# A fused attention and expert kernel: who stores the sums of w2, where 1e-6 is added, and which queue turns the last batch's x

## The chip, the cores and the metric

The kernel runs on one core of one Trainium2 chip. The metric is the device time of one execution in microseconds; the core has a matrix engine (TensorE, PE in the profile; its weight loads are listed apart as PEld), a vector engine (VectorE, DVE), an activation engine (ScalarE, ACT), a general engine (GpSimd, POOL) and a queue engine that only starts transfers (SyncE, SP). Everything is fp32, and the profile lists each fp32 matmul as two records.

## The reference

Two blocks follow each other. The first is an attention with polynomial features: `S1` and `S2` (8x32) project q and k, the outer product of the two 8-vectors gives 64 features, and no softmax is taken.

```python
def phi(x):
    a = np.einsum('rd,bhsd->bhsr', S1, x)
    b = np.einsum('rd,bhsd->bhsr', S2, x)
    return np.einsum('bhsi,bhsj->bhsij', a, b).reshape(*x.shape[:-1], r * r)
q_p, k_p = phi(q), phi(k)
kv = np.einsum('bhsf,bhsd->bhfd', k_p, v)
z = np.sum(k_p, axis=2)
num = np.einsum('bhsf,bhfd->bhsd', q_p, kv)
den = np.einsum('bhsf,bhf->bhs', q_p, z)[..., None] + 1e-06
x = (num / den)            # 4 batches, 4 heads, 1088 positions, 32 wide
```

The result, laid out as x with 4352 rows of 128, goes through a routed layer with 8 experts, in which every row meets every expert:

```python
logits = x @ w_gate; P = np.exp(logits - logits.max())
for _ in range(8):
    P /= P.sum(1, keepdims=True) + 1e-09
    P /= P.sum(0, keepdims=True) + 1e-09
    P *= N / E
for e in range(E):
    out += P[:, e:e + 1] * (np.maximum(x @ w1[e], 0.0) @ w2[e])
```

## The kernel before, in words

**Stages.** The attention of the four batches takes about the first 98 us, the routing (logits, then eight rounds of row and column sums on VectorE) some 106 to 175 us, and all the rest is expert work. Since the experts' products fill TensorE for most of the time, a generator `steps()` hands them out in small steps, and the attention and the routing call `fill(n)`, or yield `n`, at places where they would otherwise make TensorE wait: `n` is the amount of expert work put there, one unit being four matmul records of 480 columns. Up to the end of the routing, this work is on experts 0 and 1 without their routing weights, and the results stay in the tiles `kept`; they are multiplied by the weights later (`weigh_kept`). After the routing x is multiplied by an expert's weights before its first matmul (`prepare_x`, tile `xe`, on GpSimd).

**Expert work.** `items` lists pairs of a group of columns of x and an expert; an item is cut into `blocks`. In a block, `first` makes the hidden values (line 914, with the ReLU on ScalarE at 918), VectorE forms sums and differences of them (931 for groups of two tiles, 978 for groups of three), and `into` (1099) makes the second matmuls, eight steps later (`LAG`). Fast matrix multiplication saves matmuls: it needs sums of blocks of w2 as well, which GpSimd forms in `sums_of_two` (tile `ws`) and `sums_of_four` (tile `ws4`, line 242, ten instructions for 16 forms). An expert's `ws4` is formed once, stored in device memory (line 246, SyncE) and read back for later groups (line 230).

**Order.** On TensorE, VectorE, and for a part ScalarE, instructions run in the order in which the code states them. GpSimd and SyncE are ordered by the tile framework, except where `keep_in_program_order` holds an instruction in place. Each engine takes its queue in order, so a transfer on SyncE that waits for GpSimd holds up all SyncE's later transfers.

**Attention of batches 1 to 3.** `attention(b)` takes three chunks `c`. `times` multiplies the features of the queries (453), `tops(b, c)` makes numerators and denominators side by side in one PSUM tile `pn` (462), and `over(b, c)` takes the reciprocal of the denominators (475), multiplies (477) and transposes (481). In `tops`, two further matmuls (466) multiply 64 columns of ones with the tile `eps`, which holds 1e-6/128 everywhere, and so add 1e-6 to the 12 denominators of each row. `take_over` (486, 488) sends the quotient through device memory to turn it into `xT`, columns of x: one transfer out, four back. Batch 3 does this in two parts: positions 0 to 191 after `over(3, 1)` by GpSimd's queue, the rest after `over(3, 2)` by SyncE's. The logits (496) need all of `xT`.

Of the kernel before, what the change touches and what calls it, by code (L numbers as in the profile page):

```python
# [10 lines left out]
F32 = mybir.dt.float32  # L11
# [39 lines left out]
def kernel(  # L51
# [12 lines left out]
    nc = tc.nc  # L64
    P = nc.NUM_PARTITIONS
    B, H, S, D = q.shape
# [14 lines left out]
    consts = ctx.enter_context(tc.tile_pool(name="consts", bufs=1))  # L81
# [28 lines left out]
    ones = consts.tile([P, P], F32, name="ones")  # L110
# [34 lines left out]
        kvs.append(consts.tile([P, 2, 2, D + 1], F32, name=f"kvs{i}"))  # L145
        nc.gpsimd.memset(kvs[i], 0.0)

    eps = consts.tile([P, 3, H], F32, name="eps")
    nc.gpsimd.memset(eps, 1e-6 / P)

    v_slots = []
    for i in range(2):
        t = wk.tile([P, H + 1, NT + 1, D], F32, name=f"v{i}", bufs=1)
# [58 lines left out]
    stored, stored_four = {}, {}  # L212
# [13 lines left out]
    def sums_of_four(e, w2):  # L226

        ws = pools[0].tile([P, len(FORMS), FO // 4, H2], F32, tag="ws4", name="ws4")
        if e in stored_four:
            nc.sync.dma_start(out=ws, in_=stored_four[e])  # L230
            return ws

        def blocks(bs):
            b = w2[:, bs[0][1]::4, H2 * bs[0][0]:H2 * (bs[0][0] + 1)].unsqueeze(1)
            if len(bs) == 1:
                return b
            step = (bs[1][1] - bs[0][1]) * DM + (bs[1][0] - bs[0][0]) * H2
            return AP(tensor=b.tensor, offset=b.offset, ap=[b.ap[0], [step, 2], *b.ap[2:]])

        c = 0  # L240
        for ns, x, y, off in FOURS:
            tc.keep_in_program_order(nc.gpsimd.tensor_tensor(ws[:, c:c + len(ns)], blocks(x), blocks(y),  # L242
                                                             op=Alu.subtract if off else Alu.add))
            c += len(ns)
        stored_four[e] = dram.tile([P, len(FORMS), FO // 4, H2], F32, name=f"ws4{e}")
        nc.sync.dma_start(out=stored_four[e], in_=ws)
        return ws


# [205 lines left out]
    def tops(b, c):  # L455

        pn = bank()[:, 0:3 * H * (D + 1)].rearrange("p (t h d) -> p t h d", t=3, h=H)
        ph = third(phs[b % 2], c)
        for t in range(3):
            for i in range(2):  # L460
                for s in range(2):
                    nc.tensor.matmul(pn[64 * s:64 * (s + 1), t, 2 * i:2 * i + 2].rearrange("p h d -> p (h d)"),  # L462
                                     ph[:, i, s, 64 * t:64 * (t + 1)], kvs[b % 2][:, i].rearrange("p h d -> p (h d)"),
                                     start=(t == 0 and i == 0), stop=False, tile_position=(0, 64 * s))
        for s in range(2):
            nc.tensor.matmul(pn[64 * s:64 * (s + 1), :, :, D], ones[:, 0:64], eps, start=False, stop=True,
                             tile_position=(0, 64 * s))
        queries[b, c] = pn

    turned = {}  # L470
# [1 line left out]
    def over(b, c):  # L472
        pn = queries.pop((b, c))
        rc = wk.tile([P, 16], F32, tag="rc", name="rc")[:, 0:12].rearrange("p (t h) -> p t h", h=H)
        nc.vector.reciprocal(rc, pn[:, :, :, D])
        xs = wk.tile([P, 512], F32, tag="rd", name="rd")[:, 0:384].rearrange("p (h t d) -> p h t d", h=H, t=3)
        nc.vector.tensor_tensor(xs.rearrange("p h t d -> p t h d"), pn[:, :, :, 0:D],
                                rc.unsqueeze(3).to_broadcast([P, 3, H, D]), op=Alu.mult)
        if c == 0:
            turned[b] = wk.tile([P, H, W9], F32, tag="xt", name="xt", bufs=1)  # L480
        nc.vector.transpose(out=turned[b][:, :, 96 * c:96 * (c + 1)].rearrange("p h (t s) -> p h t s", t=3), in_=xs)
# [25 lines left out]
    def attention(b):  # L507


        follows = b + 1 < B  # L510
        keys_sums(b)
        times(b, 0)
        yield 2.2 if b == 1 else 2
        keys_kept(b)
        times(b, 1)
        tops(b, 0)
        if b == 1:
            transpose_q(2)
        yield 1.4
        times(b, 2)  # L520
        over(b, 0)
        tops(b, 1)
        if b == 1:
            queries_ab(2)
            repeat_a(2)
        if follows:
            repeat_b(b + 1)
        yield 1.4
        over(b, 1)
        if b + 1 == B:  # L530
            take_over(b, 0, 192, nc.gpsimd)
        yield 1.4
        tops(b, 2)
        if follows:
            transpose_k(b + 1)
        if b + 2 < B:
            load_k(b + 2)
            load_v(b + 2)
        yield 1.4
        over(b, 2)  # L540
        if b + 1 < B:
            take_over(b, 0, W9, nc.gpsimd)
        else:
            take_over(b, 192, W9, nc.sync)
        if follows:
            yield 0.7
            keys_ab(b + 1)
            yield 0.7
            if b == 1:
                transpose_q(3)  # L550
            keys_products(b + 1, 0)
            yield 1.4
            keys_products(b + 1, 1)
            if b == 1:
                queries_ab(3)
                repeat_a(3)
            yield 1.4
            keys_products(b + 1, 2)
            yield 1.4
# [10 lines left out]

    def routing():

        yield 5
        for c in range(len(chunks)):
            logits(c)
        yield 1
        for c in range(len(chunks)):
            logits_turned()
        lg = lgp[:, :, 0:E]
        mx = sk.tile([P, 1], F32, tag="mx", name="mx")  # L580
        nc.vector.tensor_reduce(out=mx, in_=lg, axis=AX.XY, op=Alu.max)
        yield 3
        pm = bank()[:, 0:P]
        for s in range(2):
            nc.tensor.matmul(pm[64 * s:64 * (s + 1)], mx.to_broadcast([P, 64]), ident, start=True, stop=True,
                             tile_position=(0, 64 * s))
        nc.vector.reduce_max(mx, pm, axis=AX.X)
        nc.vector.tensor_scalar(mx, mx, -1.0, 64 * math.log(2.0), op0=Alu.mult, op1=Alu.add)
        pw = p2s[0]
        nc.scalar.activation(out=pw[:, :, 0:E], in_=lg, func=Act.Exp, bias=mx[:, 0:1])  # L590

        step = 1.5 * 2.0 ** (23 - 149 + 64)
        nc.vector.tensor_scalar(pw[:, :, 0:E], pw[:, :, 0:E], step, step, op0=Alu.add, op1=Alu.subtract)
        for it in range(ITERS):
            rs = sk.tile([P, SA], F32, tag="rs", name="rs")
            nc.vector.reduce_sum(rs, pw, axis=AX.X)  # L596
            nc.vector.reciprocal(rs, rs)
            p1 = p1s[it % 2]
            nc.vector.scalar_tensor_tensor(p1[:, 0:SA], rs.unsqueeze(2).to_broadcast([P, SA, E]), UP,
                                           pw[:, :, 0:E], op0=Alu.mult, op1=Alu.mult)  # L600
            cs = sk.tile([P, E], F32, tag="cs", name="cs")
            nc.vector.reduce_sum(cs, p1.rearrange("p g e -> p e g"), axis=AX.X)  # L602
            yield 4.25
            pc = bank()[:, 0:E]
            for s in range(2):
                nc.tensor.matmul(pc[64 * s:64 * (s + 1)], ones[:, 0:64], cs, start=True, stop=True,
                                 tile_position=(0, 64 * s))
            cr = sk.tile([P, E], F32, tag="cr", name="cr")
            nc.vector.reciprocal(cr, pc)
            last = it == ITERS - 1  # L610
            pw = lgp if last else p2s[(it + 1) % 2]
            nc.vector.scalar_tensor_tensor(pw[:, :, 0:E], cr.unsqueeze(1).to_broadcast([P, SA, E]),
                                           float(N) / E * (1.0 if last else UP), p1[:, 0:SA],
                                           op0=Alu.mult, op1=Alu.mult)

        nc.vector.transpose(out=lgT.rearrange("p a s -> p (a s)"), in_=lgp.rearrange("p a e -> p (a e)"))
        for b in (1, 0, 2, 3):
            nc.sync.dma_start(out=pT[:, b * S:(b + 1) * S],
                                                  in_=lgT[32 * b:32 * b + E].rearrange("p a s -> p (a s)"))
# [489 lines left out]
    def steps():  # L1109

        todo, sums_at, t = {}, {}, 0
        for k in range(len(blocks) + 5):
# [5 lines left out]
            if k < len(blocks):  # L1118
# [11 lines left out]
                if q == 1 and j + 1 < first_weighted and not direct_of(j + 1) and loaded_w[j + 1][2] is None:  # L1130
                    w1, w2, _ = loaded_w[j + 1]
                    w = w1, w2, sums_of_two(items[j + 1][1], w2)
                    loaded_w.update({i: w for i in loaded_w if items[i][1] == items[j + 1][1]})
                if q == 0:
                    if weighted and 1 <= es.index(e) <= es[0] + 1:
                        weigh_kept(g, es.index(e) - 1)
                if k == len(blocks) - HELD:
                    kept_to_sums(g)
                m, step, sums_ = (four if tiles == 3 else two)(k)
# [131 lines left out]
```

## Time and profile before

| what | value |
|---|---|
| time, median of 3 (lowest to highest) | 920.12 us (920.08 to 920.75) |
| span of the profiled execution | 918.0 us |
| busy: PE, PEld | 911.2 us, 637.4 us |
| busy: DVE, ACT, POOL | 678.9 us, 421.6 us, 204.0 us |
| mean traffic of the transfers | 140 GB/s |
| granted TensorE clock | full in nearly all slices |

A busy share says how long an engine had at least one instruction in it. Matmuls overlap in the engine, so the distance from one start to the next says more on TensorE than the duration of one. The chain of waits follows the work that ended last back to its start; the waits list for each engine what ended its idle time.

### The profile page before, as it was taken

The page shows a single profiled execution, that of the slowest core. Times are in us where ns is not written, and L with a number is a line of the kernel's source. Part 1 is how long each engine was busy: PE and PEld are TensorE (multiplying, and loading weights), DVE is VectorE, ACT ScalarE, POOL GpSimd, SP SyncE. Part 2 cuts the span into 40 slices and gives each one's busy share as a digit, 9 for nine tenths or more (in the row PEclk, how much of TensorE's full clock was granted, in tenths as well). Part 3 has the DMA queues.
Part 4 walks back from the last instruction along what each step waited for, and adds up shares of the span by engine and source line. Part 5 has one row for each costly group of instructions (what it writes and reads, how often), then busy time and mean ns, then how long its engine had stood idle before and what let it go on. Part 6 is the DMA issues. An engine that isn't in the chain of part 4 may idle for free.

```text
span 918.0 us, 18893 instructions
## 1 busy us (share of the span) xinstructions
PE 911.2 (99%) x7442; PEld 637.4 (69%) x7442; DVE 678.9 (74%) x1173; ACT 421.6 (46%) x915; POOL 204.0 (22%) x212
## 2 busy tenths in 40 slices
PE   9999999999999999999999999999999999999997
PEld 6777544466666677777777777777777655556886
DVE  7678699888776798666975656956567976758665
ACT  3455555554444454444544444544445444445443
POOL 3121100175545421201210010110100243210220
PEclk9999999999999999999999999999999999999999
DMA  9994100213454535534364343454445456453640
GB/s 254 308 273 163 54 1 1 70 64 127 148 150 139 186 119 174 165 110 150 114 185 134 117 143 112 132 187 127 133 122 165 130 170 195 162 166 92 177 153 13
DMA packets 91305, 128.15 MB, mean 140 GB/s; under 512 B 25392, under 2 KB 69504, under 8 KB 86480
## 3 DMA queue, kind: packets, MB, share of 16 engines
q1 hardware_dynamic: 88384, 121.42, 42.7%
q0 software_dynamic: 1600, 5.36, 2.1%
q8 instruction: 58, 0.95, 0.4%
q10 hardware_dynamic: 1232, 0.16, 0.1%
q14 instruction: 31, 0.25, 0.1%
HBM read 107.88 MB, written 19.05 MB: 138 GB/s over the span
## 4 chain that ended last, share of the span: by engine, by line
PE 97%; DVE 2%; ACT 1%; issue 0%; POOL 0%; DVEq 0%; POOLq 0%
PE a L914 51%; PE s L1099 41%; PE a L347 1%; PE a L462 1%; PE a L114 1%; DVE hb L931 1%; PE a L314 0%; PE s L376 0%; PE a L426 0%; PE s L392 0%; DVE cs L602 0%; PE a L496 0%; PE a L392 0%; ACT hb L918 0%; DVE rs L596 0%
## 5 line engine op out<-in xcount | busy, mean ns | idle before, releaser
L914 PE MATMUL a<-xe,w 128*64 128x256 f32 (+1 forms) x2560 | 569.8, 470 | 0.0
L918 ACT ACTIVATE hb<-a 128x256 f32<-128x256 f32 (+4 forms) x408 | 195.0, 480 | 241.5 <-PE a L914 209.3
L914 PEld LDWEIGHTS a<-xe,w 128*64 128x64 f32 x2560 | 263.0, 137 | 50.8 <-issue 1.8
L918 ACT ACTIVATE hx<-a 128x256 f32<-128x256 f32 (+1 forms) x360 | 167.3, 465 | 213.5 <-PE a L914 191.6
L1099 PE MATMUL s<-hb,ws 128*64 128x256 f32 (+3 forms) x1312 | 256.1, 395 | 0.2 <-DVE hb L931 0.2
L1099 PE MATMUL s<-hx,ws 128*64 128x256 f32 x1280 | 233.9, 379 | 0.0
L978 DVE TENSOR_TENSOR hb<-hb 128x512 f32<-128x512 f32 (+1 forms) x204 | 133.5, 664 | 102.8 <-ACT hb L918 98.8
L978 DVE TENSOR_TENSOR hx<-hx 128x512 f32<-128x512 f32 (+1 forms) x204 | 149.8, 744 | 65.0 <-ACT hx L918 60.2
L1099 PEld LDWEIGHTS s<-hb,ws 128*64 128x64 f32 x1312 | 134.9, 137 | 87.8 <-issue 64.5
L678 POOL TENSOR_TENSOR xe<-xT,xe 128x768 f32<-128x768 f32 (+2 forms) x41 | 80.3, 1958 | 481.2 <-DMA xe<-pT 377.0
L1099 PEld LDWEIGHTS s<-hx,ws 128*64 128x64 f32 x1280 | 132.7, 137 | 71.6 <-issue 50.3
L914 PE MATMUL a<-xT,w 128*64 128x416 f32 (+3 forms) x512 | 119.7, 462 | 0.0
L1099 PE MATMUL s<-hb,w 128*64 128x256 f32 (+3 forms) x536 | 114.2, 408 | 0.0
L1099 PE MATMUL s<-hx,w 128*64 128x256 f32 x384 | 76.0, 379 | 0.0
L931 DVE TENSOR_TENSOR hb<-hb 128x416 f32<-128x416 f32 (+7 forms) x84 | 60.7, 723 | 18.0 <-ACT hb L918 14.0
L1099 PEld LDWEIGHTS s<-hb,w 128*64 128x64 f32 x536 | 54.1, 137 | 19.0 <-issue 6.5
L914 PEld LDWEIGHTS a<-xT,w 128*64 128x64 f32 x512 | 48.9, 137 | 25.5 <-issue 15.7
L242 POOL TENSOR_TENSOR ws<-w 128x256 f32<-128x256 f32 (+1 forms) x70 | 60.5, 899 | 8.1 <-DMA w<-in_moe_w_dram 5.2
L931 DVE TENSOR_TENSOR hx<-hx 128x256 f32<-128x256 f32 (+1 forms) x65 | 39.5, 612 | 24.0 <-ACT hx L918 22.8
L1099 PEld LDWEIGHTS s<-hx,w 128*64 128x64 f32 x384 | 40.8, 137 | 6.6
L978 DVE TENSOR_TENSOR pqg<-hb 128x512 f32<-128x512 f32 x68 | 40.5, 637 | 0.0
L978 DVE TENSOR_TENSOR pqg<-hx 128x512 f32<-128x512 f32 x68 | 35.0, 554 | 0.0
(181 smaller groups left out, 485.0 us busy)
## 6 DMA issues: line engine op xcount, KB each, us to landing
w<-in_moe_w_dram SPq DMA_DIRECT2D x82, 512.0 KB, 5.5
ws<-ws SPq DMA_DIRECT2D x34, 1024.0 KB, 5.0
xe<-pT SPq DMA_DIRECT2D x34, 384.0 KB, 4.1
ws<-ws SPq DMA_DIRECT2D x12, 512.0 KB, 3.6
ph<-qa SPq DMA_DIRECT2D x12, 288.0 KB, 4.7
rb<-qb SPq DMA_DIRECT2D x3, 1152.0 KB, 7.2
pb<-pT SPq DMA_DIRECT2D x6, 384.0 KB, 8.3
kx<-in_k_dram SPq DMA_DIRECT2D x4, 544.0 KB, 4.0
```

The costliest lines, as they stand in the source:

```text
L114: nc.tensor.matmul(warm[:, 0:P], ones, ones, start=True, stop=True)
L242: tc.keep_in_program_order(nc.gpsimd.tensor_tensor(ws[:, c:c + len(ns)], blocks(x), blocks(y), op=Alu.subtract if off else Alu.add))
L347: nc.tensor.matmul(pv[64 * s:64 * (s + 1), i], kp[0:n, H * t + h].rearrange("p i j -> p (i j)"), vx[0:n, slots[h], t, :], start=(t == 0 an ...
L462: nc.tensor.matmul(pn[64 * s:64 * (s + 1), t, 2 * i:2 * i + 2].rearrange("p h d -> p (h d)"), ph[:, i, s, 64 * t:64 * (t + 1)], kvs[b % 2] ...
L678: tc.keep_in_program_order(nc.gpsimd.tensor_tensor(out, x, pb, op=Alu.mult))
L914: nc.tensor.matmul(ph[sl], loaded_w[j][0][:, P * f + H2 * s:P * f + H2 * (s + 1)], sources[j][:, lo:hi], start=True, stop=True, tile_posit ...
L918: nc.scalar.activation(out=out, in_=ph, func=Act.Relu)
L931: nc.vector.tensor_tensor(out, a, b, op=Alu.subtract)
L978: nc.vector.tensor_tensor(out if not isinstance(out, tuple) else places(*out), places(*a), places(*b) if isinstance(b, tuple) else b, op=A ...
L1099: nc.tensor.matmul(sums[g][i][H2 * s:H2 * (s + 1), n * place:n * (place + 1)], w, x, start=c == 1, stop=c == per, tile_position=(0, H2 * s))
```

## The change

Four things change. The tile `eps` and the matmuls with it go, and `over` adds 1e-6 with a VectorE instruction before the reciprocal. The store of `ws4` moves from SyncE's queue to GpSimd's, held in program order, so that SyncE doesn't wait for GpSimd's sums. `weigh_kept` is asked for one block later in an item (at `q == 1` instead of `q == 0`), so that its transfer and its product come behind the preparation of the next item. The first part of batch 3's x goes by SyncE's queue; the expert work between `tops(3, 2)` and `over(3, 2)` shrinks from 1.4 to 0.6 units, and that ahead of the logits grows from 5 to 6.

```diff
-    eps = consts.tile([P, 3, H], F32, name="eps")
-    nc.gpsimd.memset(eps, 1e-6 / P)
...
-        nc.sync.dma_start(out=stored_four[e], in_=ws)
+        tc.keep_in_program_order(nc.gpsimd.dma_start(out=stored_four[e], in_=ws))
...
-                                     start=(t == 0 and i == 0), stop=False, tile_position=(0, 64 * s))
-        for s in range(2):
-            nc.tensor.matmul(pn[64 * s:64 * (s + 1), :, :, D], ones[:, 0:64], eps, start=False, stop=True,
-                             tile_position=(0, 64 * s))
+                                     start=(t == 0 and i == 0), stop=(t == 2 and i == 1), tile_position=(0, 64 * s))
...
-        nc.vector.reciprocal(rc, pn[:, :, :, D])
+        nc.vector.tensor_scalar_add(rc, pn[:, :, :, D], 1e-6)
+        nc.vector.reciprocal(rc, rc)
...
         if b + 1 == B:
-            take_over(b, 0, 192, nc.gpsimd)
+            take_over(b, 0, 192, nc.sync)
...
-        yield 1.4
+        yield 1.4 if follows else 0.6
         over(b, 2)
...
-        yield 5
+        yield 6
         for c in range(len(chunks)):
             logits(c)
...
-                if q == 0:
-                    if weighted and 1 <= es.index(e) <= es[0] + 1:
-                        weigh_kept(g, es.index(e) - 1)
+                if q == 1 and weighted and 1 <= es.index(e) <= es[0] + 1:
+                    weigh_kept(g, es.index(e) - 1)
```

## The prediction

> **What bounds the kernel now.** I read the page first, then the chain of waits in order of time, then the waits of TensorE alone. The page's first part and its chain name one engine:
>
> ```profile
> PE 911.2 (99%) x7442; PEld 637.4 (69%) x7442; DVE 678.9 (74%) x1173; ACT 421.6 (46%) x915; POOL 204.0 (22%) x212
> ...
> PE 97%; DVE 2%; ACT 1%; issue 0%; POOL 0%; DVEq 0%; POOLq 0%
> ```
>
> A busy share of 99% alone isn't proof, since overlapping matmuls can hide slow starts. So I look at start distances in the chain:
>
> ```profile
> 317.88 0.86 PE a L914 x4
> 319.17 0.86 PE a L914 x4
> 320.89 0.86 PE s L1099 x8
> 322.62 0.86 PE a L914 x4
> ```
>
> From 317.88 to 319.17 lie 12 records of 256 columns: 1.29 us, 107.5 ns each. From 317.88 to 322.62, the pattern's period, are 44 such records, 4.74 us, 107.7 ns each. The distance stays the same for 500 us, whatever the other engines do. So TensorE starts the next matmul when its array takes one, and only fewer or shorter matmuls shorten this stretch. The waits of TensorE over the whole run say where it does stand still:
>
> ```profile
> PE a L114 <- POOL own L116: 1.0, 1, 1.0
> PE a L392 <- ACT kvz L362: 0.6, 1, 0.6
> PE s L1099 <- DVE hb L931: 0.2, 1, 0.2
> ```
>
> The first two come in the first 15 us, which the change doesn't touch; the third, at 166 us, is all the visible idle time that an earlier partner could give back. Busy time by stage agrees (the columns are the stretch, its length and the busy time of each engine with its instructions, PE first):
>
> ```profile
> 25.00:110.00 85.00, 85.00 (x1070) 61.92 (x1066) 64.04 (x111) 39.83 (x101) 14.55 (x25) 1.00 0.69 209
> 110.00:184.00 74.00, 73.78 (x468) 33.52 (x466) 65.34 (x118) 43.95 (x91) 4.02 (x4) 1.00 0.09 23
> 184.00:317.00 133.00, 133.00 (x999) 86.97 (x996) 101.87 (x144) 58.94 (x121) 74.65 (x78) 1.00 0.41 130
> 317.00:836.00 519.00, 519.00 (x3955) 374.90 (x3952) 374.83 (x657) 230.43 (x478) 91.34 (x58) 1.00 0.47 146
> ```
>
> TensorE lacks 0.22 us between 25 and 836 us. Stalls below what this view shows are found from start distances: about 0.15 us ahead of the logits at 106.1, 0.11 behind them, 0.05 at 139.6. I put everything recoverable after 25 us at 0.3 to 0.9 us.
>
> **What the Trainium skill says.** "Perfetto Trace Analysis", section Identifying the Most-Contended Engine, warns that matmul busy time is no measure of how near an engine is to its peak; hence the step by start distances above. "VectorE: DVE Perf Modes", section The TRN2 errata, prices a matmul at max(60, 6+FD) cycles of 2.4 GHz: 109 ns for 256 columns, which the measured 107.5 ns fits, and 25 ns for the 12 columns of the `eps` product. Its VectorE row has 120 fixed cycles of 0.96 GHz for a PSUM source and 58 for an SBUF source. "DMA: Bandwidth & Descriptors", section Anatomy of one DMA, gives about 2.0 us plus bytes over 436 GB/s for a transfer issued by GpSimd: for the 1 MiB of `ws4` an estimate of 4.4 us; the trace has 4.7 to 5.1 us for the store by SyncE.
>
> **Part 1, the eps matmuls.** Nine calls of `tops` (three batches by three chunks), two matmuls each, two records per matmul: 36 records leave TensorE. Their busy time in the timeline contains latency that overlaps the next matmul, so I take start distances again:
>
> ```profile
> 34.74 0.24 PE L466 MATMUL a<-eps,ones 128*64 128x12 f32 x4
> 34.83 0.63 PE L914 MATMUL a<-xT,w 128*64 128x256 f32 x4
> ```
>
> Four records occupy 0.09 us here, and 0.09 us again at 37.34 to 37.43; the median distance behind such a record is 28 ns, or 0.11 us for four. Nine times 0.09 to 0.11 is 0.8 to 1.0 us; the sum of all distances behind the 36 records is 1.03 us. TensorE has no idle time around them to absorb the gain, so it goes to the end: minus 1.0 us. The memset of `eps` (0.12 us on GpSimd at 2.5 us) hides beside the warm-up matmuls.
>
> **Part 2, VectorE's addition.** The trace has the same pair of instructions in batch 0, and the present reciprocal from PSUM:
>
> ```profile
> 26.72 0.17 DVE L405 TENSOR_SCALAR rc<-rd 128x9 f32<-128x9 f32 x1
> 26.93 0.22 DVE L406 RECIPROCAL rc<-rc 128x9 f32<-128x9 f32 x1
> 97.11 0.23 DVE L475 RECIPROCAL rc<-a 128x12 f32<-128x12 f32 x1
> ```
>
> There the addition takes a distance of 0.21 us, from SBUF; from PSUM a little more, at most the 0.25 us of the old reciprocal to its successor. The reciprocal now reads SBUF, slightly cheaper. I take 0.23 us more per `over`, 2.1 us on VectorE for nine, three of them (0.7 us) in each batch. Queued behind the longer `over` are sums for expert blocks (931), transposes and products of the next keys (302, 331). VectorE is full in 65 to 80 us (4.8 of each 5 us), so there the 0.7 us stays until the gap of 2.73 us at 84 to 86.7, where it ends. Who waits meanwhile: the key matmuls (314) start at 75.1, some 1.7 us after their transposes end at 73.4; the key sums (347) at 82.8, 1.6 us after the product ends at 81.2. TensorE itself comes about 0.6 us earlier, so the slack falls to 0.3 us or so, and stays positive. Cost: zero; bounds 0 and 2.1 us, if every addition reached TensorE.
>
> **Part 3, batch 3's x.** Now the second part's outward transfer starts on SyncE at 98.58, its returns at 101.19 to 102.94, and TensorE's queue passes its waits for them by 104.3; the logits start at 106.11. So there is 1.8 us of slack. Afterwards the first part's quotient is ready near 94.3 (94.46 now; TensorE gains 0.7 us by then and VectorE loses 0.5). One outward transfer of 2.6 to 3 us and four returns of 0.44 us of SyncE's time put it at 99. `over(3, 2)` moves ahead by up to 0.8 units of 0.8 us, 0.64 us; its quotient comes near 98 and waits for SyncE until 99. The same steps as before, 2.6, 1.75 and 2.1 us, end near 105.1. The logits are due at 106.11 less 1.0 plus 0.2 units (0.16 us): 105.25. It just fits. Cost 0; bounds 0 and 1 us. The order of the work changes, not its amount: the units that are shifted are expert work that has to be done anyway.
>
> **Part 4, the stores.** SyncE's waits name what is relieved:
>
> ```profile
> SPq L246 <- POOL ws L242: 111.4, 7, 17.0
> ```
>
> Seven stores, 111 us of SyncE standing behind GpSimd's sums, between 175 and 308 us, in front of loads of `xe` and weights. Yet TensorE loses nothing to it in this stretch (133.00 of 133.00 us). The gain is slack alone: zero. GpSimd gets about 0.5 to 1 us more for each store (its queue's transfers at line 486 take 0.59 to 0.73 us). Behind each stands the next weighing of `xe`, which waits 6 to 8.5 us for its transfer now, and then the next sums. The tightest place is 240 us: `xe` is ready at 240.2, its item begins about 241, for 236.27 to 238.2 went to the kept product. Since `weigh_kept` moves behind and the load is no longer held up, this widens. In the last group, the kept products move by one block (4.7 us) and still end well ahead of their use. Zero.
>
> **Sum.** 920.12 - 1.0 = 919.1 us.
>
> **The rivals.** (a) The small stalls go as well: up to 0.9 us more, 918.2 to 918.6. For it: 0.2 us at 166 us hangs on the place of routing work between sums, which the shift by 0.2 units changes. Against it: the same shift can make such stalls. (b) A wait takes the removed matmuls' place: x arrives late at the logits (up to 1 us), or the additions reach TensorE (up to 2.1 us): 919.7 to 921.5, say 920.5. For it: slack of only 0.1 to 0.3 us in both reckonings. Against it: 1.8 us of slack before, and the greater lead of `over(3, 2)`. (c) GpSimd becomes the bound from 184 to 317 us: with its slack below 1 us at the tightest item, a store that took 1.5 us and stalled 0.6 us in each of seven items gives plus 4.2, 923.3 us, slower than before. Against it: GpSimd is busy 74.65 of 133 us there, and it waits for transfers between its pieces.
>
> **How the numbers follow.** The forecast, 918.6 to 919.7, has 0.62; (a) 0.12, (b) 0.18, (c) 0.08. The range takes (a) nearly whole and (b) to near its middle: 918.2 to 920.9. Faster by over 0.2% means under 918.28 us: half of (a), 0.07. Slower means over 921.96: (c) and the end of (b), 0.09. Within 0.2%: 0.84.
>
> **What would show it.** No line with `eps`; the records of PE down by 36; PE still without idle time from 25 to 836 us; the start of the logits near 105.3 us; nine additions on DVE; SyncE's wait for `ws` gone and its loads earlier. Wrong would be: a gap in front of the logits, matmuls at 75 or 83 us waiting for DVE, a wait of TensorE for GpSimd after 184 us, or a steady distance other than 107.7 ns.

## The result, and the profile after

The kernel after takes 926.00 us (median of 6 runs, 924.15 to 926.72), beside it the kernel before 920.13 us (919.50 to 920.75): 1.006 times as long, 95% interval 1.0047 to 1.0073. The forecast was 919.1 us with a range of 918.2 to 920.9, so the 5.9 us have to be explained. The profiled executions span 924.2 and 918.0 us, both at full clock.

The first and fourth parts of the page of the kernel after (busy time, and the chain that ended last by engine):

```profile
PE 913.0 (99%) x7406; PEld 534.1 (58%) x7406; DVE 688.9 (75%) x1182; ACT 421.4 (46%) x915; POOL 202.6 (22%) x213
...
PE 90%; DVE 5%; DMA 3%; issue 1%; SPq 0%; ACT 0%; ACTq 0%; DVEq 0%
```

TensorE has 36 records less, as foreseen, and its share is still 99%. But the chain now leaves it: 97% PE before, 90% now. The chain runs over VectorE and transfers for 8% of the span, so these end waits of TensorE; the 8% is the way back along the chain, not lost time. The waits of TensorE say which (engine, line, what it waited for: total, times, longest):

```profile
PE s L1094 <- DVE hx L973: 2.5, 2, 2.2
PE a L114 <- POOL own L116: 1.0, 1, 1.0
PE a L389 <- ACT kvz L359: 0.6, 1, 0.6
PE a L491 <- issue: 0.5, 1, 0.5
PE a L909 <- DVE rd L472: 0.4, 1, 0.4
PE a L311 <- DVE kT L301: 0.3, 1, 0.3
PE a L459 <- ACT hb L913: 0.3, 1, 0.3
```

The second and third are the start's, known from before. That of line 311 lies at 20.4 us, ahead of the first changed instruction of the attention, and that of line 459 at 34.6 us stands in kernels without the eps edit too (0.5 us in e2 below). The others come with the change. (Lines of the kernel after stand 3 to 5 lower than before: 1094 was 1099, the second matmuls; 973 was 978, VectorE's sums; 491 was 496, the logits; 459 was 462, `tops`; 472 was 477, the multiplication in `over`; 243 was 246, the store.) The same by stage, columns as in the prediction:

```profile
25.00:110.00 85.00, 83.61 (x1018) 61.59 (x1015) 63.77 (x116) 39.03 (x99) 11.61 (x20) 1.00 0.70 208
110.00:184.00 74.00, 73.79 (x467) 33.27 (x461) 63.83 (x119) 43.57 (x90) 0.14 (x1) 1.00 0.11 28
184.00:317.00 133.00, 130.53 (x968) 70.89 (x964) 108.55 (x142) 57.38 (x119) 77.08 (x87) 1.00 0.36 127
317.00:836.00 519.00, 519.00 (x3950) 283.59 (x3948) 376.26 (x652) 229.81 (x475) 93.39 (x57) 1.00 0.46 145
```

Nothing is lost after 317 us: TensorE is busy for all 519 us and its steady distance is unchanged (107.8 ns for 256 columns before, 107.7 after, over the whole stretch). It stands still for 2.5 us between 184 and 317 us, where it lost nothing before, and for 1.4 us before 110 us. Milestones place the loss in the same way. The logits start at 107.65 us (106.11 before), the matmul of the first sum over columns at 125.05 (121.61), the first matmul on weighted x at 187.41 (184.21), the last matmul at 918.69 (912.65). So 1.5 us are lost up to the logits, 1.7 to 1.9 at them and just behind, and nearly 3 after the routing. How many of the first 1.5 us belong to the change can't be told from this: the same attention starts the logits at 106.11 to 107.44 us in the kernel before, e2, e5, e6 and e9 below, and that of the kernel after at 105.90 in e4.

**The largest wait.** The timeline of the kernel after around its only 2.2 us wait (start, duration, engine, line, operation; in brackets the idle time before and its releaser):

```profile
195.33 0.60 POOL L243 DMA_DIRECT2D ws<-ws  x1 [0.30 <-POOL ws L239]
195.82 7.71 DVE L736 TENSOR_TENSOR z<-x,z 128x384 f32<-128x384 f32 x1 [1.93 <-ACT x L745]
195.95 1.82 POOL L673 TENSOR_TENSOR xe<-xT,xe 128x768 f32<-128x768 f32 x1
197.73 6.10 POOL L239 TENSOR_TENSOR ws<-w 128x256 f32<-128x256 f32 x10
204.44 0.65 PE L1094 MATMUL s<-hx,ws 128*64 128x256 f32 x4 [2.25 <-DVE hx L973]
```

One VectorE instruction takes 7.71 us. In the kernel before the same instruction took 0.56 us (at 192.62). It reads two SBUF operands and begins while GpSimd issues the store that the change gave it. GpSimd then works through a weighing and ten sums without slowing down (1.82 and 6.10 us), and VectorE's instruction ends only during the last of these. VectorE's next sums are what line 1094 waits for. So it isn't GpSimd that TensorE waits for here, but VectorE, which stands behind GpSimd.

### The profile page after: what moved, and what is told of

The parts are those of the page before. It is cut to its first block, busy times and chain, and to the rows that moved or that the text cites. A ratio compares the mean times of both kernels' runs of the same rounds, so it can differ in the third digit from the quotient of the medians.

```text
span 924.2 us, 18839 instructions
## 1 busy us (share of the span) xinstructions
PE 913.0 (99%) x7406; PEld 534.1 (58%) x7406; DVE 688.9 (75%) x1182; ACT 421.4 (46%) x915; POOL 202.6 (22%) x213
## 4 chain that ended last, share of the span: by engine, by line
PE 90%; DVE 5%; DMA 3%; issue 1%; SPq 0%; ACT 0%; ACTq 0%; DVEq 0%
PE a L909 48%; PE s L1094 41%; DVE hb L926 1%; DMA rb<-qb 1%; DMA kx<-in_k_dram 1%; DVE z L736 1%; DMA v<-in_v_dram 1%; PE a L344 0%; PE a L459 0%; DVE kT L299 0%; PE a L491 0%; DVE hx L973 0%; DVE rd L472 0%; DVE ph L450 0%; DVE w L736 0%
## 5 line engine op out<-in xcount | busy, mean ns | idle before, releaser
L909 PE MATMUL a<-xe,w 128*64 128x256 f32 (+1 forms) x2560 | 516.3, 470 | 0.0
L909 PEld LDWEIGHTS a<-xe,w 128*64 128x64 f32 x2560 | 200.1, 137 | 86.6 <-issue 1.6
L1094 PE MATMUL s<-hb,ws 128*64 128x256 f32 (+3 forms) x1312 | 228.6, 395 | 0.2 <-DVE hb L926 0.2
L1094 PE MATMUL s<-hx,ws 128*64 128x256 f32 x1280 | 205.4, 379 | 2.5 <-DVE hx L973 2.5
L973 DVE TENSOR_TENSOR hx<-hx 128x512 f32<-128x512 f32 (+1 forms) x204 | 160.2, 795 | 58.2 <-ACT hx L913 53.1
L1094 PEld LDWEIGHTS s<-hb,ws 128*64 128x64 f32 x1312 | 104.7, 137 | 116.3 <-issue 86.6
L1094 PEld LDWEIGHTS s<-hx,ws 128*64 128x64 f32 x1280 | 102.4, 137 | 103.4 <-issue 74.5
L1094 PE MATMUL s<-hb,w 128*64 128x256 f32 (+3 forms) x536 | 107.1, 408 | 0.0
L1094 PE MATMUL s<-hx,w 128*64 128x256 f32 x384 | 67.9, 379 | 0.0
L1094 PEld LDWEIGHTS s<-hx,w 128*64 128x64 f32 x384 | 33.2, 137 | 11.5
```

The costliest lines, as they stand in the source:

```text
L909: nc.tensor.matmul(ph[sl], loaded_w[j][0][:, P * f + H2 * s:P * f + H2 * (s + 1)], sources[j][:, lo:hi], start=True, stop=True, tile_posit ...
L973: nc.vector.tensor_tensor(out if not isinstance(out, tuple) else places(*out), places(*a), places(*b) if isinstance(b, tuple) else b, op=A ...
L1094: nc.tensor.matmul(sums[g][i][H2 * s:H2 * (s + 1), n * place:n * (place + 1)], w, x, start=c == 1, stop=c == per, tile_position=(0, H2 * s))
```

## The experiments

Each was measured beside the kernel before, whose median was 920.04, 920.27 and 920.07 us in the three sets (36 to 49 runs). They fall into four groups.

**One part at a time.** The kernel before with one part of the change:

```diff
e1_eps_alone
-    eps = consts.tile([P, 3, H], F32, name="eps")
...
-            nc.tensor.matmul(pn[64 * s:64 * (s + 1), :, :, D], ones[:, 0:64], eps, start=False, stop=True,
...
+        nc.vector.tensor_scalar_add(rc, pn[:, :, :, D], 1e-6)
+        nc.vector.reciprocal(rc, rc)
e2_store_alone
+        tc.keep_in_program_order(nc.gpsimd.dma_start(out=stored_four[e], in_=ws))
e3_x_alone
+            take_over(b, 0, 192, nc.sync)
...
+        yield 1.4 if follows else 0.6
...
+        yield 6
```

> The kernel before with the eps matmuls replaced by VectorE's addition, nothing else. Theory A (the attention stage is paced by its transfers, rb above all, and by VectorE, so that the 1.0 us that TensorE saves turns into waits there): 920.0 to 921.7 us, with new gaps of TensorE at the products with the features (34, 64 and 67 us) and behind the key matmuls (78 us). Rival B (TensorE sets the pace here, the late rb of the changed kernel's profile was an accident of the transfers): 919.1 us, no such gaps.

> The kernel before with the store of ws4 on GpSimd's queue, nothing else. Theory A (a store in GpSimd's queue ahead of a weighing and ten sums lets GpSimd keep SBUF to itself, and a VectorE sum stands until the last of them is done): one VectorE instruction of over 3 us between 184 and 320 us, TensorE waiting 2 to 3 us for it, 922.5 to 923.5 us. Rival B (that stall came from where the earlier delay of 3 us had put VectorE against GpSimd, the store has no part in it): 920.1 us, within 0.3.

> The kernel before with batch 3's first part on SyncE's queue and the shifted units, nothing else. Theory A (the second part's transfer waits in SyncE's queue for the returns of the first and then lands after the logits are due): 921 to 922 us, TensorE standing 0.7 to 1.8 us inside the logits. Rival B (the logits stall in the changed kernel only since the attention stage was late there): 919.8 to 920.4 us, no gap at the logits.

And the kernel after with its store back on SyncE:

```diff
e4_after_store_back
-        tc.keep_in_program_order(nc.gpsimd.dma_start(out=stored_four[e], in_=ws))
+        nc.sync.dma_start(out=stored_four[e], in_=ws)
```

> The changed kernel with the store of ws4 back on SyncE's queue. Theory A: the 2.9 us at 204 to 208 us go, no VectorE instruction over 3 us after 184 us: 922.8 to 923.4 us. Rival B (the collision comes from the phase): a stall of the same kind stays, 925.5 to 926.5 us.

| kernel | median us (range) | ratio, 95% interval |
|---|---|---|
| e1_eps_alone | 921.87 (919.55 to 923.40) | 1.0017, 1.0010 to 1.0023 |
| e2_store_alone | 923.61 (922.76 to 924.45) | 1.0035, 1.0023 to 1.0047 |
| e3_x_alone | 920.96 (919.81 to 921.86) | 1.0005, 0.9997 to 1.0013 |
| e4_after_store_back | 922.06 (921.35 to 923.19) | 1.0020, 1.0012 to 1.0028 |

Against 920.04 us the first three add 1.8, 3.6 and 0.9 us; their sum, 6.3, is close to the 5.9 of the whole, and putting the store back takes 3.9 off. So the store is nearly two thirds. The eps edit, which was to save 1.0 us, costs 1.8, and of batch 3's x alone it can't be told whether it costs anything: 920.96 us lies between the two ranges expected of it. e2 is 0.1 us above its theory's range and e4 0.7 below. e1 is 0.2 above, and not for the reasons given: of the places named (34, 64, 67, 78 us) only the first and last have a wait, of 0.7 and 0.3 us, and the logits weren't named.

**What in the store costs.** Three variants of the kernel before, with other stores: e5 leaves the first of the seven on SyncE's queue and puts six on GpSimd's. In e6 all stay with SyncE, each issued one item later, when its sums are long done, so that SyncE doesn't stand waiting. e9 is e6 with an 8 KB transfer of GpSimd's own added after each set of sums.

```diff
e5_first_store_back
+        if stored_four.keys() == {e}:
+            nc.sync.dma_start(out=stored_four[e], in_=ws)
+        else:
+            tc.keep_in_program_order(nc.gpsimd.dma_start(out=stored_four[e], in_=ws))
e6_store_late
     def sums_of_four(e, w2):
+        while unstored:
+            to, made = unstored.pop()
+            tc.keep_in_program_order(nc.sync.dma_start(out=to, in_=made))
...
-        nc.sync.dma_start(out=stored_four[e], in_=ws)
+        unstored.append((stored_four[e], ws))
e9_small_transfer
+        unstored.append((stored_four[e], ws))
+        small = dram.tile([P, 16], F32, name=f"small{e}")
+        tc.keep_in_program_order(nc.gpsimd.dma_start(out=small, in_=ws[:, 0, 0, 0:16]))
```

> The kernel before with six of the seven stores of ws4 on GpSimd's queue; the first stays on SyncE's. Theory A (the time is lost at one place, where the first store lets the second item's weighing and sums follow without a pause, across VectorE's sum at the end of a group): no instruction of VectorE over 5 us, no wait of TensorE for VectorE near 201 us, 919.8 to 920.6 us. Rival B (every store costs some 0.4 us): 922.5 to 923.5 us.

> The kernel before with all seven stores on SyncE's queue, but each asked for one item later, so that SyncE doesn't stand behind GpSimd's sums and the next load of xe is early, as in the changed kernel, without a transfer in GpSimd's queue. Theory A1 (the unbroken run of GpSimd's instructions shuts VectorE out; the store matters only since SyncE is free and xe comes early): a VectorE instruction of 5 to 8 us near 193 us and TensorE waiting 2 to 3 us near 201, 922.3 to 923.6 us. Rival A2 (it takes a transfer that GpSimd itself issues): no such instruction, 919.8 to 920.6 us.

> The kernel before, its stores left on SyncE's queue but issued one item later, and GpSimd issues a transfer of 128 x 16 floats (8 KB) after each set of sums. Theory S (it is the issue on GpSimd between two of its computations, of any size, that shuts VectorE out[...]): a VectorE operation of 5 to 8 us stands at the second store as with the whole store on GpSimd's queue, the matmuls wait 2 us or more for it, and the kernel takes 922.5 to 923.6 us. Rival (it takes the 1 MiB that the store reads): the longest VectorE operation behind a set of sums stays below 2.7 us and the kernel takes 920.0 to 920.6 us.

| kernel | median us | ratio, 95% interval |
|---|---|---|
| e5_first_store_back | 921.08 | 1.0009, 1.0002 to 1.0015 |
| e6_store_late | 920.18 | 0.9996, 0.9988 to 1.0004 |
| e9_small_transfer | 922.45 | 1.0026, 1.0016 to 1.0036 |

e6 and e9 have the same GpSimd computations back to back. First the timeline of e6, VectorE and GpSimd:

```profile
192.41 1.82 POOL L683 TENSOR_TENSOR xe<-xT,xe 128x768 f32<-128x768 f32 x1
193.21 1.44 DVE L746 TENSOR_TENSOR z<-x,z 128x384 f32<-128x384 f32 x1 [1.90 <-ACT x L755]
194.19 10.94 POOL L247 TENSOR_TENSOR ws<-w 128x256 f32<-128x256 f32 x10
194.57 1.22 DVE L983 TENSOR_TENSOR hx<-hx 128x512 f32<-128x512 f32 x1
195.71 1.22 DVE L983 TENSOR_TENSOR pqg<-hx 128x512 f32<-128x512 f32 x1
```

Then that of e9, with the small transfer in front:

```profile
192.41 0.60 POOL L253 DMA_DIRECT2D small<-ws  x1
193.02 1.83 POOL L685 TENSOR_TENSOR xe<-xT,xe 128x768 f32<-128x768 f32 x1
193.22 7.39 DVE L748 TENSOR_TENSOR z<-x,z 128x384 f32<-128x384 f32 x1 [1.91 <-ACT x L757]
194.80 6.12 POOL L247 TENSOR_TENSOR ws<-w 128x256 f32<-128x256 f32 x10
```

VectorE's instruction starts at the same time, 193.2 us, inside the same weighing. In e6 it gets through when the weighing ends, and from then on the two engines take turns: GpSimd's ten sums stretch to 10.94 us, VectorE's instructions to 1.2. In e9 the only difference in front of it is an issue of 0.60 us for 8 KB, and it is shut out through the weighing and nearly all ten sums, which run undisturbed in 6.12 us. TensorE then waits 1.9 us for line 985's `hx`. So it doesn't take the 1 MiB that the store reads; a transfer of 8 KB that GpSimd issues between its computations is enough.

A rival is the moment: the issue moves the weighing by 0.6 us, so that VectorE comes 0.2 us into it in e9 and 0.8 in e6. The kernel before speaks against it. There an instruction comes 0.16 us into a weighing with ten sums right behind it and no transfer ahead, and it is through just after the weighing:

```profile
197.62 1.92 POOL L678 TENSOR_TENSOR xe<-xT,xe 128x768 f32<-128x768 f32 x1 [6.03 <-DMA xe<-pT]
197.78 2.18 DVE L738 TENSOR_TENSOR z<-z,w 128x384 f32<-128x384 f32 x1
199.50 8.85 POOL L242 TENSOR_TENSOR ws<-w 128x256 f32<-128x256 f32 x10
```

So does e6: behind its third set of sums VectorE comes 0.24 us into a weighing with a second one right behind (227.77 us), and two instructions are through in 4.26 us; in e9 one alone takes 4.50 there.

And the kernel before has the long exclusion as well, where GpSimd sends off a batch's x and makes three sums behind it:

```profile
46.17 0.59 POOL L486 DMA_DIRECT2D xd<-xt  x1 [4.51 <-DVE xt L481]
46.76 2.45 DVE L931 TENSOR_TENSOR hb<-hb 128x288 f32<-128x288 f32 x1
46.78 0.75 POOL L204 TENSOR_TENSOR ws<-ws,w 128x256 f32<-128x256 f32 x1
47.47 0.73 POOL L205 TENSOR_TENSOR ws<-w 128x256 f32<-128x256 f32 x1
48.16 0.73 POOL L206 TENSOR_TENSOR ws<-w,ws 128x256 f32<-128x256 f32 x1
```

The other seven VectorE instructions of this line and shape take 0.45 or 0.46 us. In the fourteen profiles of this case a VectorE sum or product stands through two or more whole GpSimd computations 21 times: once near 47 us in each, and seven times after 184 us, in the kernel after, e2, e5 and e9. Each time it begins during an issue by GpSimd or at most 0.2 us behind it; where GpSimd's computations follow each other without one, it never happens.

SyncE's freedom from the wait, which the change wanted, brings nothing (e6). e5 loses less than e2, but more than expected: the instruction behind the first store is back at 0.56 us (at 193.94), and behind a later one TensorE waits 0.7 us for VectorE's sums. So the first store has most of the cost, not all of it.

**Where the eps edit's saving goes.** e7 takes the matmuls out and adds nothing; it leaves out 1e-6 in batches 1 to 3, with 1 in place of 0 in the padding columns of `qT` and `kT`. e8 keeps the matmuls and has VectorE add 0.0.

```diff
e7_eps_dropped
-        nc.gpsimd.memset(t[:, S:], 0.0)
+        nc.gpsimd.memset(t[:, S:], 1.0)
...
-            nc.tensor.matmul(pn[64 * s:64 * (s + 1), :, :, D], ones[:, 0:64], eps, start=False, stop=True,
e8_matmul_and_add
+        nc.vector.tensor_scalar_add(rc, pn[:, :, :, D], 0.0)
+        nc.vector.reciprocal(rc, rc)
```

> The kernel before without the eps matmuls and without the addition on VectorE; 1e-6 is left out of batches 1 to 3's denominators, and the padding columns hold 1 instead of 0. Theory A1 (VectorE's additions are what reaches TensorE, through PSUM banks that stay occupied and through batch 3's x, while the saving is real): 918.9 to 919.5 us. Rival A2 (the transfers of the queries' features pace the stage, so that the saved time turns into waits for rb): 919.8 to 920.6 us, with TensorE waiting longer near 34 us.

> The kernel before with the eps matmuls kept and an addition of 0.0 on VectorE ahead of each reciprocal, so that VectorE has the changed kernel's work and TensorE the old one. Theory A1 (each addition that lands in VectorE's full stretch delays the release of a PSUM bank or batch 3's x): 921.5 to 923.0 us, TensorE waiting behind the key matmuls at 76 us and in the logits at 107 us. Rival A2 (the additions are hidden beside TensorE's matmuls): 919.8 to 920.5 us.

e7: 919.79 us (ratio 0.9997, 0.9989 to 1.0005), e8: 920.19 us (1.0001, 0.9993 to 1.0010). Neither half does anything alone that is clear of noise: e7's interval runs from 1.0 us faster to 0.5 slower, e8's from 0.6 faster to 0.9 slower (its rival held; e7 lies between its two ranges). Together they cost 1.8 us (e1). So slack runs out: TensorE comes earlier, VectorE later, and one meets the other. Two places show it in the timeline of e1, whose profile is of the slowest of its 21 executions (923.40 us). The first is a PSUM bank:

```profile
38.72 0.16 DVE L469 TENSOR_SCALAR rc<-a 128x12 f32<-128x12 f32 x1
38.91 0.23 DVE L470 RECIPROCAL rc<-rc 128x12 f32<-128x12 f32 x1
39.18 0.56 DVE L472 TENSOR_TENSOR rd<-a,rc 128x384 f32<-128x384 f32 x1
39.79 0.55 PE L423 MATMUL a<-qT,wdq 128*64 128x192 f32 x4 [0.81 <-DVE rd L472]
40.16 0.66 PE L909 MATMUL a<-xT,w 128*64 128x288 f32 x4
```

Matmuls of line 423 write another tile with the tag `a` and use nothing that `over` produces; they wait for the multiplication of `over` because it is the last reader of `pn`. Only e1's profile has so long a wait here. In all five kernels with the additions and without the matmuls (the kernel after, e1, e4, e11, e12), matmuls of expert work wait 0.3 to 0.4 us at 76 to 78 us for the multiplication of another `over`. The second place is the logits:

```profile
101.45 0.57 SPq L481 DMA_DIRECT2D xd<-xt  x1
105.71 1.74 SPq L483 DMA_DIRECT2D xT<-xd  x4
...
108.07 1.06 PE L491 MATMUL a<-xT,wg 128*32 128x512 f32 x6
109.75 1.99 PE L491 MATMUL a<-xT,wg 128*32 128x512 f32 x18 [0.62 <-DMA xT<-xd]
```

Six records of the logits run, and the rest stand until the last part of x is there: 3.60 us from the first logits' record to the next expert matmul (111.67), 1.97 in the kernel before (106.11 to 108.08). The last part landed at 109.61 us (104.32 before), so this wait is the transfer's. Of the rest of what e1's profile lost, a part belongs to no edit: the transfer into `rb` that lets `tops` start at 34 us ends at a different time in every profile (VectorE's product with it starts from 32.7 to 34.1 us in all fourteen, those with the old matmuls too).

**Queue, order, and the kernel mended.** e10 is the kernel before with batch 3's first part on SyncE's queue and nothing else. e12 is e1 with leads of 0.6 and 7. e11 is the kernel after with e6's late stores and a lead of 7 instead of 6.

```diff
e10_queue_alone
+            take_over(b, 0, 192, nc.sync)
e12_eps_real_lead (against e1_eps_alone)
+        yield 1.4 if follows else 0.6
...
-        yield 5
+        yield 7
e11_after_late_lead (against the kernel after)
-        tc.keep_in_program_order(nc.gpsimd.dma_start(out=stored_four[e], in_=ws))
+        unstored.append((stored_four[e], ws))
...
-        yield 6
+        yield 7
```

> The kernel before with batch 3's first part of x written by SyncE's queue, and the two leads as before. The leads have been seen to move no instruction up to the logits, so all that this third part of the change does should be the queue: the same 920 to 921 us as all of the third part alone gave. Rival (the small excess of that run came from the expert work moved behind the logits by the second lead): 920.1 us here.

> The kernel before with the removed 1e-6 matmuls and VectorE's addition, and leads of 0.6 and 7, which move two steps of expert work ahead of the logits and leave the order behind them. Theory (1.2 to 1.6 us of what this edit alone lost is the logits' wait for batch 3's x): no wait over 0.3 us at the logits, 920.0 to 920.9 us. Rival (the loss sits in the bank waits of 35 to 80 us alone): the kernel stays at 921.5 to 922.3 us though the logits' wait is gone.

> The kernel after with its stores on SyncE's queue, each issued one item later so that it need not wait for its sums, and the second lead at 7 in place of 6, which does move two steps of expert work ahead of the logits. If the two losses are the store on GpSimd's queue and the logits' wait for batch 3's x, both are gone and what is left is the addition's bank waits near 35 to 42 us against the matmuls saved: 919.5 to 920.6 us. Rival (the losses only move: bank waits and later column sums take the place of the logits' wait): 921.5 to 922.5 us, as with the stores put back and nothing else.

e10: 920.83 us (ratio 1.0006, 0.9998 to 1.0015), as e3 had with the leads too; that the leads of 0.6 and 6 do nothing fits, but the interval holds zero and the rival isn't excluded by it. e12: 920.17 us (1.0004, 0.9996 to 1.0012), 1.7 us less than e1. Its timeline at the logits:

```profile
109.52 2.04 PE L491 MATMUL a<-xT,wg 128*32 128x512 f32 x24
111.49 0.57 PE L909 MATMUL a<-xT,w 128*64 128x416 f32 x2
```

All 24 records in one piece, 1.97 us, so the wait is gone and the time with it. What remains of TensorE's waits in e12 is as long as the saving of the removed matmuls (its last matmul is at 912.86 us, 912.65 before); the first of them is that behind `rb`, which belongs to no edit:

```profile
PE a L459 <- ACT hb L913: 0.6, 1, 0.6
...
PE s L1094 <- DVE hb L926: 0.4, 1, 0.4
PE a L909 <- DVE rd L472: 0.3, 1, 0.3
```

e11: 920.06 us (0.9999, 0.9990 to 1.0007). Everything the change lost is back, as was expected; e11 changes store and lead together, e4 and e12 one of them each. In the stage of the stores TensorE is full again (columns as before):

```profile
184.00:317.00 133.00, 133.00 (x994) 74.95 (x992) 106.96 (x144) 58.84 (x121) 78.06 (x79) 1.00 0.38 131
```

But it isn't faster than the kernel before. No kernel here that computes all of the reference beats that.

## Why the prediction was wrong

**The bound.** Right: TensorE at 107.7 ns per record for 500 us, and there nothing changed.

**Part 1, the eps matmuls: minus 1.0 us.** The records went as reckoned (36 less). Alone, the saving may well be real: e7's median is 0.5 us below that of its kernel before, 1.0 us is at the edge of its interval, and in its trace the logits start 0.87 us earlier than before (105.24 us). "TensorE has no idle time around them to absorb the gain, so it goes to the end" is what failed: with the addition nothing of it is left (e12), or less than nothing (e1). No visible idle time before an edit doesn't mean no limit just behind it.

**Part 2, VectorE's addition: cost zero.** Its size was right: 0.19 us from the addition's start to the reciprocal's, 0.23 forecast. (That the reciprocal would be slightly cheaper from SBUF was not: 0.23 us, median of nine, 0.22 before.) Alone it is hidden (e8). At the key matmuls the slack did stay positive: it was 1.3 us before, since they start at 74.73 us, not 1.7, and 0.4 us after (transposes to 75.46, matmuls from 75.83). But this step looked only at who uses what VectorE makes, at 75 and 83 us. It left out who uses the bank that VectorE reads: `pn` is free only after `over` has multiplied, and matmuls at 39.8 us in e1 and near 78 us in the kernel after (0.4 us, line 909) wait for it.

**Part 3, batch 3's x: cost zero.** The slack of 1.8 us before was read rightly: the last return landed at 104.32 us. The sum against it failed. Counted from the end of `tops(3, 2)` (96.98 and 98.64 us), x is whole after 7.34 us in the kernel before and after 10.46 in the kernel after. Of these 3.1 us, 0.8 are the last transposition, which ends 2.37 us behind `tops` (1.57 before; 2.13 in e8, with the additions alone); 0.5 a wait in SyncE's queue behind the first part's returns; 1.0 the outward transfer, 3.6 us from its issue to the first return (2.6 before); 0.8 the last return, 2.6 us from issue to landing (1.8 before). The logits are due 0.1 us earlier. So x lands at 109.10 us, 1.45 us after the logits have started; six records that don't need it run, the seventh starts at 109.19, and all the logits take 3.46 us in place of 1.97.

Two terms of the forecast failed. The outward transfer was taken at 2.6 us. And the quotient was to be ready 7.25 us ahead of the logits (near 98 and at 105.25); it was 6.6 us ahead (101.01 and 107.65), since the leads that this relied on, "`over(3, 2)` moves ahead by up to 0.8 units, 0.64 us" and "the logits are due at 106.11 less 1.0 plus 0.2 units", moved nothing. Expert work is handed out in steps, here of 0.87 units (416 of 480 columns), and neither change of 0.8 nor of 1 moves an instruction of TensorE up to the logits. The order there is the same in both kernels but for the eps rows. e12 and e11, whose lead of 7 moves two steps ahead of the logits, have no wait. These two steps are 16 records and 2.79 us, so a unit here is about eight records and 1.6 us, not four and 0.8, since the second matmuls come with it. Nor did the sum fit in its own terms: 99 and 2.6, 1.75 and 2.1 us give 105.45, behind the 105.25 at which the logits were due. Rival (b) named this wait and gave it "up to 1 us"; it was 1.5.

**Part 4, the stores: zero.** This is the step that cost most, 3.6 us alone (e2). Its reckoning of GpSimd held: 0.60 us for an issue (0.5 to 1 forecast), and TensorE nowhere waits for GpSimd after 184 us. Part 4 asked only what waits for GpSimd, not whom GpSimd's instructions keep out. Rival (c) had the right stage and side of the result, but not the mechanism: it had GpSimd as the bound, whereas TensorE waits for VectorE. That its 4.2 us come near the 3.6 is luck. The trace before held a hint, the 2.45 us at 46.76. The Trainium skill, page "SBUF — State Buffer", section Who interferes with whom, says that a VectorE instruction with two SBUF inputs contends with a GpSimd instruction that reads SBUF, that the ports they share are an exclusive lock, and that the order of issue decides who blocks. Read for this change, it would have pointed at VectorE's sums behind each store, and the traces agree that VectorE stands while GpSimd works. It wouldn't have given the size: one GpSimd instruction is at most 1.82 us there, and the trace has 7.71 us through ten of them.

**What stays open.** That a transfer issued by GpSimd brings the long exclusion is shown (e9 against e6); why the engines take turns without it and not behind it isn't. Nor is it known what makes the outward transfer of x take 2.6 us in one kernel and 4.3 in another. It goes with what was issued just ahead: with the first part on GpSimd's queue it took 2.6 to 2.7 us where it was issued ahead of the first part's returns (before, e2, e5, e6, e9; 3.2 in e8, with the least lead), 4.1 to 4.3 behind one or two of them (e1, e7, e12), and behind all four on SyncE's queue 2.5 (e3, e10) to 3.6 (the kernel after, e4). No run changes that order alone. Why the last return takes 2.6 to 2.8 us in the five kernels with the whole eps edit, and 1.8 to 2.0 in all others, isn't known either. The later `weigh_kept` was not tried alone; it is in e11, which has no loss left.

## What to carry to other kernels

Before moving a transfer to a compute engine's queue, ask whom that engine's instructions keep out, not only whether it has time: where VectorE and GpSimd both worked on SBUF operands here, the time hung on their taking turns, and a transfer issued by GpSimd ended that. When an edit takes work from the bounding engine and gives it to another, reckon both shifts against the same slack, and count as waiting also those who need the buffer that the other engine reads. A lead given in units of work moves nothing until it passes the next step: compare the order of the instructions, not the number.

## What the runs showed of the hardware that was not expected

- A VectorE instruction of 0.56 us with two SBUF operands took 7.39 to 7.71 us when it met GpSimd's computations behind a transfer issued by GpSimd (the kernel after, e2, e9). Such instructions took 3.99 to 4.50 us through two weighings (the kernel after, e2, e5, e9), and 2.39 to 2.68 us in place of 0.46 through three sums near 47 us in all fourteen profiles. Without the transfer it took 1.44 us (e6), with GpSimd's sums slowed from 6.1 to 10.9 us for ten.
- The exclusion doesn't need a large transfer: 7.39 us with 8 KB (e9), 7.59 with 1 MiB (e2). In the whole time 8 KB cost 2.4 us and 1 MiB 3.6, with intervals that overlap; whether size adds something isn't settled.
- In the kernel after the VectorE instruction's record starts at 195.82 us, ahead of the weighing's at 195.95, and yet it is the one that waits. The page named above lets the order of issue decide; the starts of the records don't show that order, or it doesn't hold behind GpSimd's transfers, and no run tells which.
- PEld's busy time fell from 637 to 534 us. In the steady stretch it was 374.90 us for 3952 weight loads before and 283.59 for 3948 after, in the same 519 us, so it isn't a measure of work here.
